# Batch 0's sketches with tokens stationary, a block-diagonal kv and a late division, in a sketched-attention and FFN kernel

## The chip, the cores and the metric

The kernel runs on one core of a Trainium2 chip. The metric is the time of one execution in microseconds (us) on the device; smaller is better. The core has five engines that run side by side, each through its own list of instructions in order, and meet through semaphores: TensorE (PE in the profile; its weight loads are the row PEld), VectorE (DVE), ScalarE (ACT), GpSimd (POOL) and SyncE (SP, which here only starts DMA transfers). SBUF is the working memory of 128 partitions; PSUM, in eight banks, receives TensorE's results.

## What is computed

Four batches of attention with polynomial sketches, then a feed-forward network over all 4352 tokens:

```
q, k, v: [4 batches, 4 heads, 1088 tokens, 32]    S1, S2: [8, 32]
phi(x) = (S1 x) outer (S2 x)                      -> 64 features per token
q_p, k_p = phi(q), phi(k)
kv  = sum over tokens of k_p (x) v                -> [batch, head, 64, 32]
z   = sum over tokens of k_p
num = q_p . kv        den = q_p . z + 1e-6
x   = (num / den), heads side by side             -> [4352, 128]
h   = x @ w_in        [128, 2048]
out = (h - tanh(h)) @ w_out     [2048, 128]
```

Inputs and output are float32. The denominator is not taken from the 64 features: with the Gram matrix of k's two sketches, den is a sum of eight products per token and head.

## The kernel before

**An order written out by hand.** Every operation is recorded with `P.add(engines, function, r=..., w=..., name=...)`. A long string, `TABLE` (line 26), then lists the operations in the order in which they are to stand: a number (the operation), a letter (v VectorE, a ScalarE, g GpSimd, t TensorE, s SyncE) and the buffer picked. `plan` (line 175) reads it, and `sync` (line 238) adds the semaphore waits that the data need. The tokens `f` and `F` are filler matmuls on zeros (lines 429 and 430), which write a bank that nobody reads. So the table decides which engine takes an operation and what stands in front of it; nothing is moved at run time.

**Names.** An operation's name says its step and batch. `kT0` are the transposes of k (line 536), `stt` that of S1 and S2 (542), `wab`, `wqd`, `wqc` the arranged S weights (545 to 555), `ksk0` the k sketch (581), `kab0` its move to SBUF (593), `gram0`, `gm0`, `scmm0`, `wqs0`, `sc0` the denominator's weights (608 to 638), `w0.0` to `w0.2` the products of the k sketches in three thirds (648), `kvmm0` the sum over tokens (663), `kvd`, `kvt`, `kvb` copies and a transpose of kv (672 on). For q: `qT` (573), `qsk` (706 and 759), `abc` its transpose to SBUF, `m`, `den`, `rd`, `aq` the denominator, its reciprocal and the division (712 to 718, 776 to 784), `qp` the products, `qpT` their transposes, `num` the numerator (737 and 818), `x` the copy into `xT`, the FFN's input. For the weights: `wi0` to `wi3` and `wo0` to `wo3` are casts to bf16, `wit` transposes of `wi` on TensorE (887), `wiT` their copies, `wc` a product of the two weights (901), used for the linear part of h - tanh(h). In the FFN, `h3.5` is group 3, block 5 of the first matmul (923), `th` the tanh on ScalarE (927), `dg` a part of h - tanh(h) on VectorE (932), `o` the second matmul (944, 948), `ot` and `st` the last transpose and store. Loads are `lk`, `lq`, `lv`, `lwi`, `lwo`, `sin` (line 465); `lv0.2` is the third load of v in batch 0.

**Stages.** The 4352 tokens go through the FFN in ten groups of columns (`GCOLS`: 384, 352, 352, six of 512, 192); each has 16 blocks `h`, 16 tanhs and 18 `o` matmuls. Group 0 needs only the first 384 columns of batch 0. Those are the first 12 of q's 34 token blocks, which `q_heads` (line 698) treats apart from the rest so that `h0.0` can start before the other tokens are through. The attention of batches 1 to 3, and the rest of batch 0 (`q_front(0, 3, 9)`), is interleaved with the FFN by the table.

**Batch 0's k side before** (line 575 on): the weights `wab` stay in the array and k streams through; the sketch comes out with features in partitions, and two VectorE transposes bring tokens back into partitions (`kab0.0`, `kab0.1`). Then the three products, three parts of `kvmm0`, and two ways out of the result: `kv_heads` (690) makes the block-diagonal form that the first numerator takes (`kvh`, a transpose, and `kve`, a product with a mask), `kv_tail` (672) the form that the rest takes (`kvd0`, `kvt0`, `kvb0`).

**Batch 0's first q before**: one matmul `qsk0.0`, a transpose `abc0.0`, then `m0.0`, `den0.0`, `rd0.0`, `aq0.0`: the quotient goes into one sketch factor ahead of the products `qph0`.

**The lock.** Operations with `lock=True` on VectorE and GpSimd are kept apart: each waits for the last locked one on the other engine (line 228). So two such products never run at the same time.

**Loads.** A load marked big waits until at most `CAP` (1.45 MB) is under way. Before, the first S load is issued by ScalarE, all others by SyncE.

Of the kernel before, what the change touches and what calls it, by code (L numbers as in the profile page):

```python
# [4 lines left out]
B, H, S, D = 4, 4, 1088, 32  # L5
# [5 lines left out]
NB = 9  # L11
# [15 lines left out]
0v 56g 16s 15a 10g 1g 18s 58g 2g 17s 4v 30s 19s 29s 21s 23s 50v:0 51v 20s 5v 52v 22s 54v 53v 55g f F F F F F F F F F F  # L27
66t:0 6v 64g 24s 67t 12g 65g 68t 60g 69v:0 3g 13g 25s 70v 57g f F F F 71t:0 84v 76g:0 26s 107v 72a:0 f F 73t 74a 27s
8g 77v:1 7g F F F 85t:0 35s 75v 78g:2 111t:0 86v:0 79t:1 112v:1 80t 87g:0 81t 9g 88v:0 113g:1 34s 229a 82v 89v:0 59g
90g:0 114v:1 108a:0 28s F F F F 109t 230a 91v:0 237t:0 95v:1 49s 231a 238t 115v:1 83v 240t:1 31s 232a 92v:0 116g:1  # L30
239a 96v:1 F 241t 117g:2 32s 110v:0 93t:2 242a 97t:1 33s 94a 124v:0 98a f F F 249t:0 125v 233g 251t:1 42s 253t:2
250a:0 38s 126t:0 118v:0 119g:0 252a:1 254a:2 255t:0 43s 281t:0 127v:1 257t:1 256a:3 282t 40s 283t 128v 259t:2 234g
258a:4 261t:0 120v 41s 129t:0 260a:5 263t:1 61g 235g 284t 39s 130a:1 265t:2 262a:6 285t 131t 14g 264a:7 286t 236v
267t:0 37s 266a:8 287t 269t:1 288t 132v:0 268a:9 134v:3 289t 243t:2 270a:10 271t:0 244t 36s 273t:1 135v:4 272a:11 290t
245t 274a:12 275t:0 121t:0 105s 136v:0 276a:13 103s 159v:0 277t:0 44s 279t:1 123a 246t 46s 133v 160v 278a:14 137t:2
247a 45s 138t 122v 139t 248v 161t:0 106s 143v 140a:1 280a:15 48s 304t:0 291t 141t 162v:0 305a:16 104s 292t 306t:1 163v
308t:0 142a:1 310t:2 144t:0 307a:17 169g:1 309a:18 100s 312t:0 311a:19 314t:1 293t 101s 145v:0 313a:20 316t:2 294t
295t 315a:21 296t 47s 318t:0 317a:22 320t:1 297t 319a:23 298t 146g:0 322t:2 164t:0 321a:24 299v:0 324t:0 323a:25
326t:1 147v:0 300s 165a:0 328t:2 325a:26 166t 336t:0 148v:0 327a:27 99s 337t 330t:0 167v:1 329a:0 149v:0 332t:1 102s
338t 331a:1 339t 168v 150g:1 178v 301s 334t:2 340t 333a:2 341t 359t:0 302s 335a:28 361t:1 342t 360a:29 363t:2 303s  # L40
179t:0 362a:3 152g:2 151v:1 364a:30 365t:0 343t 367t:1 344t 366a:31 180v:1 369t:2 345t 368a:4 371t:0 154g:0 346t
370a:5 373t:1 347t 372a:32 348t 375t:2 153v 349t 374a:33 377t:0 350t 376a:6 351t 181g:1 379t:1 352t 378a:7 155v 381t:2
380a:8 383t:0 353t 382a:9 385t:1 156t:0 354v:1 384a:10 386a:11 182v:1 355s 356s 391t:0 357s 392t 158v 157a 387t:0 393t
358s 389t:1 394t 388a:12 171v:2 414t:2 395t 390a:13 416t:0 415a:14 396t 418t:1 183v:1 397t 194v:0 417a:15 398t 184g:1
420t:2 399t 419a:16 422t:0 195v 185g:1 400t 401t 421a:17 424t:1 213v 402t 403t 423a:18 404t 426t:2 405t 425a:19 406t
170g:3 428t:0 427a:20 407t 408t 430t:1 429a:21 432t:2 409v:2 196t:0 431a:22 186v:0 410s 62g 187g:2 433a:23 434t:0 411s
436t:1 197v:1 438t:2 435a:24 412s 172t:2 198v 437a:25 173t 413s 204g:4 199t:0 439a:26 174t 200a:1 440t:0 201t 175v:0
442t:1 441a:27 446t:0 11g 202v:0 444t:2 63g 203v 176t 443a:0 189g:0 188v 447t 469t:0 445a:1 448t 471t:1 177v:2 470a:2
449t 473t:2 472a:28 205g:0 475t:0 190v 214t:0 474a:29 476a:3 477t:1 479t:2 215v:0 206g:1 450t 478a:30 451t 481t:0
480a:31 483t:1 452t 482a:4 453t 485t:2 454t 484a:5 216v:0 455t 487t:0 486a:32 217v:0 489t:1 191t:0 488a:33 218v:0  # L50
490a:6 219v:0 220g:1 491t:0 192v 493t:1 495t:2 492a:7 456t 457t 193v 222g:2 494a:8 497t:0 458t 496a:9 459t 221v:1
499t:1 460t 498a:10 524t:2 461t 224g:0 500a:11 223v 462t 463t 525a:12 527t:0 530t:1 464v:0 207t:0 528a:13 208t 526v
531a:14 465s 533t:2 529v 501t:0 466s 532v 502t 534a:15 225v 536t:0 467s 503t 539t:1 537a:16 504t 468s 535v 505t
540a:17 538v 542t:2 506t 545t:0 541v 543a:18 507t 548t:1 546a:19 508t 544v 509t 549a:20 551t:2 547v 510t 511t 552a:21
550v 554t:0 512t 557t:1 553v 555a:22 513t 560t:2 558a:23 514t 556v 515t 561a:24 563t:0 559v 516t 517t 564a:25 562v
566t:1 518t 569t:2 565v 567a:26 209t 519v:1 570a:27 599t:0 568v 520s 572t:0 571v 600a:0 602t:1 573t 521s 605t:2 603a:1
601v 574t 522s 575t 606a:2 608t:0 604v 576t 523s 577t 609a:28 607v 611t:1 578t 614t:2 610v 612a:29 579t 580t 210v:1
617t:0 615a:3 581t 613v 582t 618a:30 583t 616v 620t:1 584t 619v 623t:2 621a:31 585t 626t:0 624a:4 586t 622v 587t
627a:5 588t 625v 629t:1 211t 628v 632t:2 630a:32 589t 212v:3 635t:0 633a:33 226t:0 631v 636a:6 634v 590v:2 638t:1 637v
591s 647t:0 228a 227v 641t:0 592s 644t:2 639a:7 648t 593s 649t 642a:8 670t:0 640v 671t 594s 645a:9 674t:1 643v 650t  # L60
# [269 lines left out]
def bass_polysketch_attn__then__act_tanh_shrink_kernel(  # L330
# [311 lines left out]
    wvs = {}  # L642
# [399 lines left out]
```

## Time and profile before

| | us |
|---|---|
| median of 3 timed runs | 105.1 (104.66 to 106.0) |
| span of the profiled execution | 102.0 |
| start of the first FFN matmul in it | 17.28 |
| last FFN matmul issued | 98.33 |

The span runs from the first to the last instruction that the profile holds; the timed runs are longer by what lies around it. The profile lists, for each engine, groups of instructions with their busy time, their mean duration in ns, and how long the engine sat idle in front of them and for whom. A duration is that of one instruction from start to end. TensorE's matmuls are pipelined, so its rate is read from the distance of their starts: two 512-column bf16 matmuls start 216 ns apart, two 384-column ones 162 ns. A float32 matmul shows as two instructions, called passes here. On VectorE and ScalarE an instruction starts some 0.07 to 0.11 us before the one in front has ended; the distance of starts is called the pitch.

When the loads of batch 0 and of the weights landed, in us from the start of the span, from the trace's semaphores:

```
k, first half 3.34   second half 4.35     S1 3.69   S2 4.53
q, first part 6.27   second part 5.82 and 6.73
v, by heads   7.68, 8.02, 8.40, 10.96
w_in quarters 12.02, 12.69, 13.29, 13.95
w_out, first quarter 16.95
```

The S loads were issued at 0.74 (ScalarE) and 1.65 us (SyncE) and took 0.64 and 0.68 us to issue.

### The profile page before, as it was taken

Reading aid. Unit: us, or ns where it says so; the run is one execution under the profiler, and the core shown is the slowest. Engines: PE = TensorE matmul, PEld = TensorE weight load, DVE = VectorE, ACT = ScalarE, POOL = GpSimd, SP = SyncE. Lnnn points to the kernel's source line nnn. Section 1 sums busy time; section 2 is a strip of 40 time slices with the busy share of each in tenths; the row PEclk is TensorE's granted clock in tenths of the full one; section 3 lists DMA queues with packets and bytes.
Section 4 is the critical chain, followed back from the end, with each engine's and each line's share of the span. In section 5 each row is a group of like instructions: output and inputs, shape, how many; then the busy total and the mean of one; then the engine's idle time right before and its main releaser. Section 6 shows DMA issues by size and latency. Waiting matters only on the chain.

```text
span 102.0 us, 3040 instructions
## 1 busy us (share of the span) xinstructions
PE 96.4 (94%) x1260; PEld 48.4 (47%) x1260; DVE 79.7 (78%) x145; ACT 79.1 (78%) x157; POOL 35.8 (35%) x54
## 2 busy tenths in 40 slices
PE   5989889999999999999999999999999999999960
PEld 2343556476645454545634454444454444445650
DVE  1668899699948996977787789687899789999430
ACT  4001297996589996999899697999997999999940
POOL 3066939900053891299893880000000000000000
PEclk9999999999999999999999999999999999999999
DMA  2897999989995831303100004305100320601555
GB/s 90 230 291 171 318 310 262 297 263 325 313 278 174 237 58 21 48 8 53 24 0 6 0 0 63 46 0 79 24 0 10 55 45 0 98 5 17 82 75 81
DMA packets 25917, 11.37 MB, mean 111 GB/s; under 512 B 19120, under 2 KB 23600, under 8 KB 25904
## 3 DMA queue, kind: packets, MB, share of 16 engines
q1 hardware_dynamic: 24288, 10.98, 41.6%
q10 hardware_dynamic: 1616, 0.20, 1.3%
q8 instruction: 10, 0.16, 0.7%
q14 instruction: 3, 0.02, 0.1%
HBM read 8.95 MB, written 2.23 MB: 110 GB/s over the span
## 4 chain that ended last, share of the span: by engine, by line
PE 68%; POOL 12%; DVE 11%; DMA 3%; issue 2%; SPq 0%; DVEq 0%
PE psb L923 25%; PE psb L944 25%; POOL w L648 6%; POOL qp L802 4%; PE psb L818 4%; PE psb L581 3%; DMA kL<-in_k_dram 3%; PE psb L663 3%; PE psb L948 2%; PE psb L759 2%; PE psb L737 2%; DVE ot L953 2%; DVE qT L573 1%; DVE qp L724 1%; DVE rd L782 1%
## 5 line engine op out<-in xcount | busy, mean ns | idle before, releaser
L923 PE MATMUL psb<-xT,wi 128*128 128x512 bf16 (+3 forms) x160 | 48.8, 349 | 0.2 <-DVE th L932 0.2
L927 ACT ACTIVATE th<-psb 128x512 bf16<-128x512 f32 (+3 forms) x77 | 40.4, 598 | 2.7 <-PE psb L923 2.2
L944 PE MATMUL psb<-th,wo 128*128 128x512 bf16 (+3 forms) x90 | 26.4, 343 | 0.0
L923 PEld LDWEIGHTS psb<-xT,wi 128*128 128x128 bf16 x160 | 14.7, 97 | 23.1 <-ACT th L927 4.1
L927 ACT ACTIVATE wo_f<-psb 128x512 bf16<-128x512 f32 (+2 forms) x28 | 16.6, 629 | 1.5 <-PE psb L923 1.3
L802 POOL TENSOR_TENSOR qp<-ap,abc 128x768 f32<-128x768 f32 x11 | 16.5, 1514 | 3.7 <-DVE ap L784 3.5
L927 ACT ACTIVATE wi_f<-psb 128x512 bf16<-128x512 f32 (+3 forms) x31 | 16.6, 622 | 0.9 <-PE psb L923 0.7
L932 DVE TENSOR_TENSOR th<-psb,th 128x320 bf16<-128x320 f32 (+2 forms) x24 | 13.4, 565 | 1.9 <-ACT th L927 1.2
L648 POOL TENSOR_TENSOR w<-abk 128x768 f32<-128x768 f32 x7 | 10.6, 1516 | 9.2 <-DVE abk L593 8.2
L944 PEld LDWEIGHTS psb<-th,wo 128*128 128x128 bf16 x90 | 8.8, 100 | 5.2
L807 DVE STREAM_TRANSPOSE qpT<-qp 128x768 f32<-128x768 f32 x11 | 10.4, 956 | 0.8 <-POOL qp L802 0.8
L944 PE MATMUL psb<-wo_f,wo 128*128 128x512 bf16 (+1 forms) x32 | 10.9, 363 | 0.0
L944 PE MATMUL psb<-wi_f,wo 128*128 128x512 bf16 (+2 forms) x38 | 10.3, 344 | 0.0
L953 DVE STREAM_TRANSPOSE ot<-psb 128x512 f32<-128x512 f32 (+3 forms) x10 | 6.3, 628 | 3.4 <-PE psb L944 3.3
L430 PE MATMUL psb<-zz 128*128 128x512 bf16 x24 | 8.1, 465 | 0.0
L932 DVE TENSOR_TENSOR wi_f<-psb,wi_f 128x192 bf16<-128x192 f32 (+1 forms) x12 | 6.1, 510 | 1.6 <-ACT wi_f L927 0.9
L932 DVE TENSOR_TENSOR wo_f<-psb,wo_f 128x320 bf16<-128x320 f32 (+2 forms) x12 | 6.8, 572 | 0.7 <-ACT wo_f L927 0.3
L536 DVE STREAM_TRANSPOSE kT<-kL 128x576 f32<-128x576 f32 (+3 forms) x10 | 5.8, 605 | 1.5 <-DMA kL<-in_k_dram 1.4
L764 DVE STREAM_TRANSPOSE abc<-psb 128x1152 f32<-128x1152 f32 (+1 forms) x4 | 5.1, 1274 | 1.9 <-PE psb L759 1.8
L818 PE MATMUL psb<-qpT,kvb 32*32 32x288 f32 (+1 forms) x256 | 6.1, 392 | 0.0
L663 PE MATMUL psb<-w,vL 128*32 128x64 f32 x288 | 5.2, 221 | 0.3 <-DMA vL<-in_v_dram 0.3
L573 DVE STREAM_TRANSPOSE qT<-qL 128x1088 f32<-128x1088 f32 (+2 forms) x5 | 5.2, 1055 | 0.0
(89 smaller groups left out, 98.2 us busy)
## 6 DMA issues: line engine op xcount, KB each, us to landing
vL<-in_v_dram SPq DMA_DIRECT2D x16, 144.0 KB, 4.0
kL<-in_k_dram SPq DMA_DIRECT2D x8, 272.0 KB, 3.3
qL<-in_q_dram SPq DMA_DIRECT2D x6, 272.0 KB, 4.6
wi_f<-in_moe_w_in_dram SPq DMA_DIRECT2D x4, 256.0 KB, 5.6
wo_f<-in_moe_w_out_dram SPq DMA_DIRECT2D x4, 256.0 KB, 5.0
out_dram<-ot SPq DMA_DIRECT2D x14, 64.0 KB, 2.0
out_dram<-ot SPq DMA_DIRECT2D x8, 48.0 KB, 2.8
qL<-in_q_dram SPq DMA_DIRECT2D x2, 176.0 KB, 3.4
```

Of the source, the lines that this page charges most:

```text
L430: "F": lambda e, n: e.matmul(bank(3), zz.ap[:, 0:128], zz.ap[:, None, 128:384].to_broadcast([128, 2, 256]), start=True, stop=True)}, zop)
L573: P.add(_v((z - a) * 32), lambda e, n: e.transpose(tv.ap, vals[0].ap), r=vals, w=[tv] if b < 3 else [x[2] for x in qTv[0][1:]], name=f"qT{ ...
L648: P.add({**_v(768), **_gt(768)}, lambda e, n: e.tensor_tensor(out=wv.ap.rearrange("p (x i j) -> p x i j", i=8, j=8), in0=abh(0)[:, :, :, N ...
L663: i = e.matmul(pv[b].ap[h * 32:(h + 1) * 32, 0:64], vL[b][:, h, blk * 32:(blk + 1) * 32], wvs[b, p].ap[:, (bi * 4 + h) * 64:(bi * 4 + h + ...
L802: P.add({**_v(cn * 256), **_gt(cn * 256)}, lambda e, n, qp=qp, c0=c0, cn=cn: e.tensor_tensor(out=qp.ap[:, 0:cn * 256].rearrange("p (x i j) ...
L807: P.add(_v(cn * 256), lambda e, n, qp=qp, o0=o0, cn=cn: e.transpose(qt.ap[:, o0 * 256:(o0 + cn) * 256], qp.ap[:, 0:cn * 256]), r=[qp], w=[ ...
L818: i = e.matmul(psa4[h * 32:(h + 1) * 32, g, 0:nb * 32], kvb.ap[g * 32:(g + 1) * 32, x, h * 32:(h + 1) * 32], qq[g * 32:(g + 1) * 32, 0:nb, ...
L923: P.add(_mm(n_), lambda e, n, jb=jb, hv=hv: e.matmul(hv.ap[:, jb % m * 512:jb % m * 512 + n_], wi[jb // 4].ap[:, (jb % 4) * 128:(jb % 4 + ...
L927: act = P.add(_a(n_ * m), lambda e, n, hv=hv, th=th: e.activation(out=th.ap.rearrange("p (u x) -> p u x", u=m)[:, :, 0:n_], in_=hv.ap.rear ...
L932: P.add(_vp(gc * m), lambda e, n, hv=hv, th=th: e.tensor_tensor(out=th.ap.rearrange("p (u x) -> p u x", u=m)[:, :, 0:gc], in0=hv.ap.rearra ...
L944: fn = lambda e, n, x=x, st=st, sp_=sp_: e.matmul(ov.ap[:, 0:n_], wo[x // 4].ap[:, x % 4, :], ths[x][0].ap[:, ths[x][1] * 512:ths[x][1] * ...
L953: P.add(_vp(n_), lambda e, n: e.transpose(ot.ap[:, 0:n_], ov.ap[:, 0:n_]), r=[ov], w=[ot], name=f"ot{gi}")
```

## The change

1. **k sketch of batch 0** (`sketch0`): k's blocks of 32 tokens become the stationary operand and the S weights `wqdc`, block-diagonal over the heads, the moving one, 64 columns at a time. The result has tokens in partitions. 36 matmuls in three parts `kst0.*`, each followed by a copy from PSUM to SBUF (`kab0.*`; parts 0 on VectorE, 1 and 2 on ScalarE). The k transposes write k in another layout, for all batches; the sketches of batches 1 to 3 read it in one run.
2. **Products** (`outer0`, `qph0`): on VectorE the first factor is read from PSUM, and such a product no longer takes part in the lock. `lock` becomes a list of engines. `w0.0` is on VectorE, `w0.1` and `w0.2` on GpSimd; one of the two `qph0` is on each. `scx` and `dg` lose the lock too.
3. **kv** (`kv0`): v's blocks move and `w` is stationary, so that the sum is formed block-diagonal at once, after one matmul of zeros that clears the bank: 72 matmuls in three parts, a copy `kvd0` (ScalarE). `kvh` and `kve` are gone. The other form is made by one float32 matmul `kvr0` with a matrix of ones and zeros (`ehf`, built by `eh` on VectorE and `ehf` on ScalarE) and the copy `kvb0`.
4. **First q** (`q_heads`): 48 matmuls `qab0` and 48 `csk0` with tokens stationary replace `qsk0.0` and the transpose `abc0.0`. The products take the undivided sketch; the reciprocal is brought into the numerator's layout by a transpose (`rdt0`) and multiplied in when the numerator is copied out (`x0.0.*`, both on VectorE).
5. **Loads**: S2, one load of v (`lv0.2`) and two of w_in (`lwi0`, `lwi2`) are issued by ScalarE; the other three loads of v go ahead of q's second part on SyncE. `stt` no longer waits for a k transpose.
6. **The table** is new as a whole. There are 13 fillers and `kvz0` (the matmul of zeros) instead of 28 fillers. Of the four `wit`, only `wit1` stands ahead of `h0.0`. On VectorE `stt` is the first transpose, ahead of those of k; `abc0.3` stands ahead of the two `x0.0`. On ScalarE the order is `kab0.2`, `gm0`, `wqs0`, `lwi2` (behind q's second part), `wi0`, `kvd0`, `wi1`, `th0.0`, `th0.1`, `wi2`, `th0.7`, `th0.4`, `wi3`. `wiT0` and `wiT1` move from ScalarE to VectorE; of the products of batches 1 to 3, six go from GpSimd to VectorE and five the other way.

The diff, cut to its core:

```diff
-            if o.lock and e in lastl:
+            if e in o.lock:
                 d = lastl["gpsimd" if e == "vector" else "vector"]
...
-                    kTv[b][r0].ap.rearrange("p (j u t r) -> p r j u t", u=2, t=32, r=2)[:, r0:r1, e_:9, e_, :],
+                    kTv[b][r0].ap.rearrange("p (j t r u) -> p r j t u", u=2, t=32, r=2)[:, r0:r1, e_:9, :, e_],
...
+    def sketch0():
+        for p in range(3):
+            def sk(e, n, p=p):
+                for blk in range(3):
+                    for c in range(4):
+                        i = e.matmul(pk0[p].ap[c * 32:(c + 1) * 32, blk * 64:(blk + 1) * 64],
+                                     kTv[0][0].ap[:, ((p * 3 + blk) * 4 + c) * 32:((p * 3 + blk) * 4 + c + 1) * 32], wqdc.ap, start=True, stop=True, skip_group_check=True)
+                return i
...
+    def outer0():
...
+                a = sbuf if n == "gpsimd" else pk0[p].ap[:, 0:192].rearrange("p (k x i) -> p x k i", x=2, i=8)
...
+            P.add({**_vp(768), **_gt(768)}, mul, r=[pk0[p], ab0v[p]], w=[wv], name=f"w0.{p}", lock=("gpsimd",))
+
+    def kv0():
...
+                for x in range(2):
+                    for h in range(4):
+                        i = e.matmul(pvd.ap[h * 32:(h + 1) * 32, x * 128 + h * 32:x * 128 + (h + 1) * 32],
+                                     wvs[0, p].ap[:, (bi * 4 + h) * 64 + x * 32:(bi * 4 + h) * 64 + (x + 1) * 32],
+                                     vL[0][:, h, blk * 32:(blk + 1) * 32],
+                                     start=False, stop=(blk == 8), skip_group_check=True)
...
+        P.add(_pe(480, 185.0), lambda e, n: e.matmul(
+            pr.ap[:, 0:256], ehf.ap, kvd0.ap.rearrange("p x c -> p (x c)"), start=True, stop=True),
+            r=[kvd0, ehf], w=[pr], mode="128x128", name="kvr0")
...
+        def sk(e, n, dst, f0, f1):
+            for c in range(nx):
+                for h in range(H):
+                    i = e.matmul(dst.ap[h * 32:(h + 1) * 32, c * (f1 - f0):(c + 1) * (f1 - f0)], qt_.ap[:, c * 32:(c + 1) * 32],
+                                 wqd[:, h, f0:f1], start=True, stop=True, skip_group_check=True)
+            return i
...
+        P.add(_v(nx * 32), lambda e, n: e.transpose(
+            rdt.ap, rd.ap[:, 0:nx, None].to_broadcast([128, nx, 32])), r=[rd], w=[rdt], name="rdt0")
...
+            ot_p.seed(2, P.add(_vp((z - a) * 32), lambda e, n, a=a, z=z, xv=xv, pn=pn: e.tensor_tensor(
+                out=xv.ap, in0=pn.ap[:, 0:(z - a) * 32], in1=rdt.ap[:, a * 32:z * 32], op=ALU.mult),
+                r=[pn, rdt], w=[xv], name=f"x0.0.{j}"))
```

## The prediction

> **What bounds the kernel now.** I read the page's shares and slices, then the busy time in three stages, then the chain of waits up to the first FFN matmul (`h0.0`, 17.28 us), then single engines inside that stretch.
>
> The first two fences are from the page and from busy time by stage (columns: stretch and its length, then busy us and instructions of PE, PEld, DVE, ACT, POOL, then PEclk, DMA share, GB/s).
>
> ```profile
> PE 96.4 (94%) x1260; PEld 48.4 (47%) x1260; DVE 79.7 (78%) x145; ACT 79.1 (78%) x157; POOL 35.8 (35%) x54
> ...
> PEclk9999999999999999999999999999999999999999
> DMA  2897999989995831303100004305100320601555
> ```
> ```profile
> 0.00:17.28 17.28, 15.30 (x222) 7.68 (x223) 12.58 (x31) 6.57 (x12) 9.29 (x29) 1.00 0.79 237
> 17.28:25.00 7.72, 7.72 (x141) 4.53 (x141) 6.70 (x12) 6.33 (x16) 3.21 (x6) 1.00 0.94 295
> 25.00:98.40 73.40, 73.20 (x901) 36.17 (x899) 60.02 (x103) 66.23 (x130) 23.32 (x20) 1.00 0.29 63
> ```
>
> Behind `h0.0` TensorE is never idle for long: 80.9 of 81.1 us busy, while ACT has 8.5 us of slack. In front of it TensorE's 15.3 us are mostly fillers (28 on zeros) while it waits. So the time is when `h0.0` starts, plus TensorE's work behind it, plus a tail (last transpose and store) of 3.6 us, which the change leaves alone. The next fence is the chain of waits (start, us, what):
>
> ```profile
> 6.91 0.45 DVE abk L593
> ...
> 7.44 1.52 POOL w L648
> 8.98 0.97 DVE w L648
> 10.02 1.51 POOL w L648
> 11.54 0.34 POOL m L712
> ...
> 12.06 0.59 POOL m L776
> ...
> 13.13 1.03 DVE qp L724 x2
> ...
> 15.19 1.69 PE psb L737 x8
> ```
>
> Three batch-0 products run one behind the other over POOL, DVE, POOL, because locked products on the two engines wait for each other; the denominators queue behind them on POOL. Then come q's products, transposes and the numerator. Last, ACT and TensorE rows in order of time:
>
> ```profile
> 12.05 0.62 ACT L359 CAST wi<-wi_f 128x512 bf16<-128x512 f32 x1 [3.38 <-DMA wi_f<-in_moe_w_in_dram]
> 12.57 0.37 ACT L359 COPY kvd<-psb 128x256 f32<-128x256 f32 x1
> ```
> ```profile
> 7.41 0.34 PE L608 MATMUL psb<-abk 128*32 128x32 f32 x17
> ...
> 11.01 1.21 PE L663 MATMUL psb<-w,vL 128*32 128x64 f32 x72 [0.27 <-DMA vL<-in_v_dram]
> ```
>
> The first pair shows that wi arrived only at 12 us. From the second come prices: 72 passes of 64 columns start within 1.21-0.22 = 0.99 us (14 ns each), 17 of 32 columns within 0.34-0.20 = 0.14 us (9 ns each).
>
> **The front, step by step** (new starts in span time).
>
> *S and k.* Both S loads are now issued by ACT, 0.64 us each, the second at 1.4. S landed 2.9 us after its issue before (3.7 and 4.5), so now at 4.3; k's halves landed at 3.35 and 4.35. The S transpose now stands first on DVE, ahead of all k transposes, two of which ran at 3.4 before. So everything behind it begins at 4.3: S (pitch 0.17), `wqd`, newly on DVE (0.17), and four k transposes (pitch 0.40, 0.33, 0.40, 0.33) end at 6.15, against 5.46. I charge this in full: the sketch starts at 6.2, not 5.51. If S lands at 3.7, it starts at 5.4.
>
> *k sketch.* 36 matmuls, two passes each like L663, 64 columns: 72 x 14 ns = 1.0 us, ready in thirds at 6.8, 7.1, 7.45. Plain copies (0.33 us, row 128x192 from PSUM) replace two transposes: `kab0.1` on ACT to 7.2, `kab0.0` on DVE to 7.5, `kab0.2` on ACT, behind a DMA issue and `ehf`, to 8.0.
>
> *q's first sketch.* `qab0` is 48 matmuls of 16 columns, `csk0` 48 of 8. No row has these; nearest are 9 ns a pass at 32 columns, 14 at 64. I take 9: 96 x 9 = 0.85 us each. Bounds 0.6 and 1.35; the upper would delay `h0.0` by about 0.5 each. [...]
>
> *Products.* `w0.0` on DVE reads one factor from PSUM. Price: 768 elements took 0.96 us from SBUF, L932's 640 with a PSUM factor 0.82, the same rate. It runs 7.55 to 8.5 without the lock. POOL makes `w0.1` 7.3 to 8.8 and `w0.2` to 10.3 (1.51 each): last product 10.3, not 11.54. No row shows such products side by side; the bounds are 0 and one whole DVE product (+1.0). I take 0: beside DVE's transposes L573, L709 and L764 POOL's w stayed at 1.51, those being single-stream too.
>
> *kv.* 72 matmuls of 32 columns: 144 x 9 = 1.3 us in thirds; the last, behind `csk0` and `w0.2`, gives its result at 11.4. This replaces 0.99 us, the transpose `kvh` (0.25) and the mask `kve` (0.36). v was whole at 10.96 before; its loads now go ahead of q's second part, and three fourths had landed by 8.4 even before: I take 8.4, not binding. `kvd0` copies on ACT (0.37) to 11.9.
>
> *Numerator.* Unchanged at 1.69 us: 12.0 to 13.7. m, den, rd and the new `rdt0` (0.55, like L730) cost 1.3 us of DVE, beside kv and numerator. But DVE is FIFO: `abc0.3` (0.99), then two dividing copies (0.33 each) end at 14.25. Loads moved from SP to ACT free SP by 0.5 to 0.6 us each and add a wait: `lwi2` stands on ACT until q's second part lands, with `wi0` and `kvd0` behind it; `kvd0` also stands behind the cast of wi's first quarter. If that lands by 11, nothing is lost; it is issued at about 7 on a queue of its own, not 6.5 behind v, and I take 11. `h0.0` at 14.4: **2.9 us earlier**.
>
> **What is paid behind it.** Three of four wi transposes (before, all lay in the waits of the front) come behind `h0.0`: 3 x 4 x 56 ns plus weights = 0.72 us. `kvr0`, a 256-column f32 matmul, replaces `kvt0` and is also behind: two passes at 163 ns x 256/192, plus 0.1 of a first load and 0.09 of a mode switch = 0.53. **+1.25 us.** ACT now casts wi2 and wi3 (0.52 pitch) among the first tanhs (0.385 pitch against 0.32 of TensorE for an h and an o), and POOL reaches wo0 only after qp. By order, TensorE waits for batch 1's k transpose (0.6), tanhs (0.7) and x0.3 (0.3) soon after: 1.2 to 1.6 us. Before, all its waits behind `h0.0` came to about 1.3 us (kvmm 0.6, qsk1 0.4), nearly all after 25 us, and that part is reordered. I take +0.4 net, between 0 and +1.5. Fewer POOL products and the new kT layout: 0, since `ksk` keeps its 8 matmuls of 288 columns (0.76 us now; bound -0.1 for all three).
>
> **Sum:** -2.9 + 1.25 + 0.4 = -1.25 us; span 102.0 to 100.8. The profiled span stands 3.1 below the median of 105.1; with the same 3.1 around it, 103.85, rounded to **103.8 us**.
>
> **Rivals.**
> 1. *Charges not met* (0.34). S lands at 3.7: -0.8. Or tanh pacing leaves TensorE gaps that the wi transposes fill: -0.7 to -0.95. For: a small load's 2.9 us may be mostly waiting beside k's stream; ACT's pitch exceeds TensorE's. Against: both earlier S loads took the same 2.9; the new order has its own waits. One of them gives 103.0, both 102.2.
> 2. *Weights bind* (0.10): wi's first quarter lands at 12.0 as before, `kvd0` ends at 12.95, numerator 13.05 to 14.75, `h0.0` at 15.2. For: v's last fourth and wi straggled then, at 130 GB/s from 8.5 to 10 us. -2.1 + 1.25 + 0.4: 104.7.
> 3. *Slower: the clock falls* (0.16). The first fillers start 427 ns apart and, from 4.75 us, 216: TensorE ran at half speed for its first 3.6 busy us. After 5.3 us the change drops all but two of 17 fillers, and the front's matmuls, in 128*32 tiles, load the array less than fillers do. If the clock falls at about 8 us, the 2.3 us of `qsk0.3` and numerator double, the small matmuls perhaps too (+1.9), and the FFN's first 3.6 us do half their work (+1.8): +4.1 to +6.0, net +2.9 to +4.8, about 109. It decides if the clock is still down at `h0.0`. Against: no gap of the new order exceeds about 1 us, and the row never leaves full speed. [...]
> 4. *The products don't overlap* (0.04), so the freed lock does nothing: `h0.0` at 15.4, 104.8. For: two streams each; against: the transposes above.
>
> **Numbers.** Forecast 0.36, its own range 102.8 to 104.9. From 2% (103.0 and 107.2; about what runs of 104.66 to 106.0 can tell): faster is a quarter of the forecast, 0.10, and most of rival 1, 0.29: 0.39. Slower is most of rival 3, 0.15, and 0.01 of rival 2's tail: 0.16. Within: 0.45. The range 101.8 to 106.8 leaves out rival 3 and the edge of rival 1.
>
> **What would show it.** `stt` at 4.3 and the first sketch at 6.2; passes of 9 ns; POOL's two w back to back at 1.51 beside DVE's; `h0.0` at 14.4 (15.2 with `kvd` standing behind `wi`: rival 2); 216 ns between 512-column matmuls throughout; TensorE waits of 1.2 to 1.6 us soon after `h0.0`. Wrong if `h0.0` comes after 15.5, or waits behind it grow by over 1.5 us.

## The result: 116.4 us, slower, and the profile after

| | before | after |
|---|---|---|
| median of the timed runs, us | 105.55 (104.66 to 106.16) | 116.38 (116.15 to 116.75) |
| span of the profiled execution | 102.0 | 114.3 |
| first FFN matmul `h0.0` starts | 17.28 | 26.19 |
| from there to the start of the last `h` matmul | 79.97 | 82.84 |
| the rest of the span | 4.75 | 5.27 |

The ratio is 1.105 (95% interval 1.097 to 1.113). Of the 12.3 us between the spans, 8.9 came in front of `h0.0`, where 2.9 were to be saved, and 2.9 behind it, where 1.65 were forecast. The last 0.5 lies in the tail, which the prediction took as unchanged.

The first fence is from the page of after, in the order of the one before: busy time of the engines, the granted clock and the DMA share by slices, and the queue that carries instructions. The second is busy time by stage, with the columns of the prediction's second fence.

```profile
PE 99.2 (87%) x1548; PEld 52.4 (46%) x1548; DVE 83.3 (73%) x149; ACT 79.5 (70%) x157; POOL 34.2 (30%) x50
...
PEclk9999755558999999999999999999999999999999
DMA  3988499899850000004026300400700410014455
...
q8 instruction: 12, 0.20, 0.8%
```
```profile
0.00:26.19 26.19, 16.43 (x496) 11.03 (x497) 11.01 (x29) 4.07 (x9) 7.02 (x26) 0.75 0.82 253
26.19:45.00 18.81, 17.80 (x327) 10.21 (x327) 16.03 (x27) 15.98 (x41) 11.86 (x13) 0.99 0.34 106
45.00:110.00 65.00, 64.59 (x726) 31.05 (x725) 55.92 (x94) 59.45 (x108) 15.34 (x12) 1.00 0.22 36
```

Three things stand here. TensorE ran 496 matmul records and 497 weight loads in front of `h0.0`, where before had 222 and 223. The clock, at full speed in the row of before throughout, is at half from 13.1 to 26.75 us. And no other engine was busy for even half of the front. The chain of waits of after shows what the time goes to (start, us, what):

```profile
1.43 3.73 DMA sin<-in_S_dram
...
6.04 1.48 DVE kT L544 x3
...
7.57 1.21 PE psb L697 x72
...
10.42 0.27 PE psb L727 x7
10.69 2.63 issue
...
15.22 2.65 issue
...
20.34 1.69 issue
22.02 0.86 PE psb L815 x6
22.88 2.87 PE psb L792 x8
```

Three times TensorE waits in the middle of an operation for nothing that the profile shows: 2.63 + 2.65 + 1.69 = 6.97 us. Its data were there. The timeline around the first gap (start, us, engine, operation, idle before) shows POOL finishing its products meanwhile and `kvmm0` (L727) picking up where it had stopped, after 10 records of a run that all had their inputs:

```profile
10.05 1.51 POOL L712 TENSOR_TENSOR w<-abk 128x768 f32<-128x768 f32 x1
...
10.41 0.28 PE L727 MATMUL psb<-vL,w 128*32 128x32 f32 x10
...
13.32 0.39 PE L727 MATMUL psb<-vL,w 128*32 128x32 f32 x13 [2.63 <-issue]
```

Counting the trace's TensorE records in order of start (matmuls, weight loads, and the few records of TensorE's own semaphore waits, 7 of the 1000 in front of `h0.0`) gives the places. The gaps lie right behind the 449th, the 705th and the 961st record: 256 apart. The instruction queue q8 moves packets of 16,384 bytes, and one lands shortly ahead of the end of each gap. There are 12 of them in this execution and 10 in that of before, as many as there are marks (records 194, 450, 706 and so on, 256 apart) in their 3115 and 2539 records:

```
                            after                     before
record 194 starts           8.66                      10.17
record 450 starts          13.32  (gap 2.63)          17.03  (no gap)
record 706 starts          17.87  (gap 2.65)          24.14  (no gap)
record 962 starts          22.02  (gap 1.69)          28.86  (no gap)
q8 packets                 10.95-11.84, 15.45-16.50,  11.96-12.93, 17.88-18.86,
                           19.52-20.62, 23.77-25.40   26.51-27.39, 30.39-32.07
h0.0 is record             1001                       452
```

TensorE resumes 1.48, 1.37 and 1.40 us after a packet's end; in every run below that has a gap at such a mark, it resumes 1.3 to 1.5 us after one. In after the first four packets start 2.29, 2.13, 1.65 and 1.75 us behind the records 194, 450, 706 and 962, in before 1.79, 0.84, 2.37 and 1.53. So the author's reading, from these counts and times alone: a packet is a block of 256 of TensorE's instructions; a packet goes with each mark that TensorE passes; and where TensorE reaches the next mark before the block has landed, it stands. What lies between the queue and TensorE the trace does not show. Before ran 256 records in 4.7 to 7.1 us, and every block was in time, the closest by 1.47 us (27.39 against 28.86). The sketches of after run 256 records in about 2 us (8.66 to 10.69), and every block up to `h0.0` is late.

Theory A was that reading: records per microsecond against blocks, with the lower clock as its consequence. The rivals: the clock falls for want of work and is itself the main loss; the late start of the sketch (7.57 against 5.51 us) is; or the rest of the chain (loads, products, a new order) is.

### The profile page after: what moved, and what is told of

Read it like the earlier page. It is cut to its first block, busy times and chain, and to the rows that moved or that the text cites. A ratio compares the mean times of both kernels' runs of the same rounds, so it can differ in the third digit from the quotient of the medians.

```text
span 114.3 us, 3613 instructions
## 1 busy us (share of the span) xinstructions
PE 99.2 (87%) x1548; PEld 52.4 (46%) x1548; DVE 83.3 (73%) x149; ACT 79.5 (70%) x157; POOL 34.2 (30%) x50
## 4 chain that ended last, share of the span: by engine, by line
PE 73%; DVE 9%; issue 7%; POOL 4%; DMA 3%; ACTq 1%; ACT 0%
PE psb L977 25%; PE psb L998 24%; DVE kT L544 6%; PE psb L874 4%; PE psb L815 3%; DMA sin<-in_S_dram 3%; PE psb L665 3%; POOL qp L858 3%; PE psb L792 3%; PE psb L1002 2%; PE psb L756 2%; PE psb L727 2%; PE psb L589 1%; PE psb L697 1%; DVE xT L360 1%
## 5 line engine op out<-in xcount | busy, mean ns | idle before, releaser
L981 ACT ACTIVATE th<-psb 128x512 bf16<-128x512 f32 (+3 forms) x78 | 43.2, 596 | 9.4 <-PE psb L977 8.8
L981 ACT ACTIVATE wo_f<-psb 128x512 bf16<-128x512 f32 (+3 forms) x29 | 17.2, 610 | 1.3 <-PE psb L977 1.0
L986 DVE TENSOR_TENSOR th<-psb,th 128x320 bf16<-128x320 f32 (+2 forms) x26 | 14.6, 566 | 3.2 <-ACT th L981 2.5
L858 POOL TENSOR_TENSOR qp<-ap,abc 128x768 f32<-128x768 f32 x8 | 12.0, 1512 | 1.3 <-DVE qp L858 1.1
L998 PE MATMUL psb<-wi_f,wo 128*128 128x512 bf16 (+2 forms) x33 | 11.5, 355 | 0.0
L998 PE MATMUL psb<-wo_f,wo 128*128 128x512 bf16 (+2 forms) x36 | 10.9, 342 | 0.0
L544 DVE STREAM_TRANSPOSE kT<-kL 128x576 f32<-128x576 f32 (+3 forms) x10 | 8.7, 936 | 0.0
L986 DVE TENSOR_TENSOR wo_f<-psb,wo_f 128x192 bf16<-128x192 f32 (+2 forms) x10 | 5.7, 568 | 1.1 <-ACT wo_f L981 0.6
L986 DVE TENSOR_TENSOR wi_f<-psb,wi_f 128x192 bf16<-128x192 f32 (+2 forms) x12 | 6.0, 507 | 0.4
L815 PE MATMUL psb<-qT,wq 32*32 32x288 f32 (+1 forms) x128 | 4.1, 441 | 1.7 <-issue 1.7
```

The lines of the kernel that those rows point to most:

```text
L544: P.add(_v(nb * 32 * (r1 - r0)), lambda e, n, e_=e_, nb=nb, r0=r0, r1=r1: e.transpose(kTv[b][r0].ap.rearrange("p (j t r u) -> p r j t u", ...
L815: i = e.matmul(psa4[g * 32:(g + 1) * 32, h, 0:sn], wq[h * 32:(h + 1) * 32, :], qv4(b)[h * 32:(h + 1) * 32, s0:s1, g, :], start=True, stop= ...
L858: P.add({**_v(cn * 256), **_gt(cn * 256)}, lambda e, n, qp=qp, c0=c0, cn=cn: e.tensor_tensor(out=qp.ap[:, 0:cn * 256].rearrange("p (x i j) ...
L981: act = P.add(_a(n_ * m), lambda e, n, hv=hv, th=th: e.activation(out=th.ap.rearrange("p (u x) -> p u x", u=m)[:, :, 0:n_], in_=hv.ap.rear ...
L986: P.add(_vp(gc * m), lambda e, n, hv=hv, th=th: e.tensor_tensor(out=th.ap.rearrange("p (u x) -> p u x", u=m)[:, :, 0:gc], in0=hv.ap.rearra ...
L998: fn = lambda e, n, x=x, st=st, sp_=sp_: e.matmul(ov.ap[:, 0:n_], wo[x // 4].ap[:, x % 4, :], ths[x][0].ap[:, ths[x][1] * 512:ths[x][1] * ...
```

## Experiments

Each median is compared with runs of before on the same chip, whose medians were 105.0, 104.7, 104.5 and 104.8 in the four batches.

**1. After, with q's two sketches in wide matmuls** (`e1_wide_q`), 360 records fewer:

```diff
-            for c in range(nx):
-                for h in range(H):
-                    i = e.matmul(dst.ap[h * 32:(h + 1) * 32, c * (f1 - f0):(c + 1) * (f1 - f0)], qt_.ap[:, c * 32:(c + 1) * 32],
-                                 wqd[:, h, f0:f1], start=True, stop=True, skip_group_check=True)
+            w_ = H * (f1 - f0)
+            for c in range(nx // 4):
+                i = e.matmul(dst.ap[:, c * w_:(c + 1) * w_], qt_.ap[:, c * 128:(c + 1) * 128],
+                             wqd[:, :, f0:f1], start=True, stop=True, skip_group_check=True)
```

> The changed kernel with q's two sketches in 3 + 3 wide matmuls (128 tokens stationary, all four heads at once) in place of 48 + 48 small ones: the same products, 360 fewer TensorE records ahead of h0.0, which comes as about the 640th instead of the 1000th. The values of batch 0's first 384 tokens land in another layout, so those output rows are not the reference's.
> Theory A (TensorE runs out of fetched instructions; each of the three gaps of 2.6, 2.7 and 1.7 us stands where another 256 instructions are needed): one gap is left, at the 449th record; the other two go. h0.0 between 18.5 and 21.5 us instead of 26.2, time 108 to 111.5 us against 116.4.
> Theory B (the small tiles or the clock hold TensorE, the gaps are its restart): the clock falls as before, gaps stay in number though not in place; 114.5 to 117 us.
> Theory C (the chain of S, w0 and kvd0 is late, TensorE merely waits for it): h0.0 stays at 25.5 to 26.5, 115.5 to 117 us.

Measured: three runs of 108.97 to 109.39 us and one of 106.8. In the profiled one (108.97) `h0.0` starts at 19.16 instead of 26.19, as record 641, and no gap is left at a mark of 256: record 450 comes only 3.9 us after record 194. That is A, and `h0.0` comes seven microseconds earlier. What stays is the clock, in the page's slices and in TensorE's timeline:

```profile
PEclk9995555999999999999999999999999999999999
```
```profile
5.15 0.27 PE L433 MATMUL psb<-zz 128*128 128x256 bf16 x1
7.41 1.10 PE L697 MATMUL psb<-wqd,kT 128*32 128x64 f32 x54 [1.98 <-DVE kT L544]
```

The 1.98 us in which TensorE waits for k's transposes lie in the stretch from 4.71 to 8.12, behind which the clock is at half until 18.36. The run of 106.8 kept the full clock; the other three had a mean of 0.952. So, by that one run, the clock costs this kernel 2.4 us, and without either fault it stands 1.8 us above before.

**2. Before, with many small matmuls added** (`e2_more_small`): each filler from the 12th on becomes a short filler and 16 matmuls of 32 columns on zeros, 544 records more.

```diff
+        i = plain["f"](e, n)
+        for j in range(16):
+            g = j % 4
+            i = e.matmul(bank(3)[g * 32:(g + 1) * 32, 256:288], zz.ap[:, 0:32], zz.ap[:, 0:32], start=True, stop=True, skip_group_check=True)
```

> The kernel before, with each of the 17 fillers behind the first 11 cut to half its columns and followed by 16 matmuls of 32 columns in 32-column tiles: 544 more records in the first 17 us, nothing else changed, no result changed. Each filler lasts about as long as before (0.1 us of columns and 16 passes of about 9 ns).
> Theory A: idle stretches of TensorE that wait for nothing, right behind the 449th, the 705th and perhaps the 961st record, 1 to 2.7 us each; h0.0 at 20 to 25 us instead of 17.3; 108.5 to 114 us against 105.5.
> Theory B: small tiles cost their own passes only; h0.0 17.3 to 17.8, 105.3 to 106.2 us.
> Theory C: the kernel before has the early S and the old chain, so nothing moves: 105.3 to 106 us.

Measured: 110.61 us, ratio 1.044 (1.035 to 1.052). The chain of waits:

```profile
10.38 0.21 PE psb L429
10.60 0.20 PE psb L441 x13
10.79 2.45 issue
13.24 0.20 PE psb L441 x3
```

The 449th record, done at 10.79, brings a gap of 2.45 us in a kernel in which nothing else of the change is present, and the 705th one of 0.59. `h0.0` moves from 17.28 to 23.81, but the gaps are only 3.0 of these 6.5 us. The added work has a price of its own: a short filler and its sixteen matmuls start 0.42 us from the next such pair, where one filler took 0.22. And the clock, at half from 14.30 to 17.71 us, has `kvmm0` take 2.15 us instead of 1.21. So the place and the length of the gaps speak for A, not the whole of the delay. A holds from both sides: take records away and the gaps go, add records and they come.

**3. After, with records spent early** (`e3_burn_early`): 8 small matmuls behind each of the first 11 fillers, 176 records in a stretch that was meant to be one where TensorE only waits.

> The changed kernel with 8 small matmuls added behind each of the first 11 fillers: 176 more records before 5.5 us, when TensorE has nothing else to do; no result changed.
> Theory A, with the next block asked for when the 193rd record is passed: that is passed at about 5.5 us instead of 8.7, so the third block is there at about 10 instead of 13.3, and the gaps come earlier in the program: h0.0 2 to 3 us earlier (23 to 24.5 us) with more instructions, time 113 to 114.5 us against 116.4. (A with blocks that are never asked for early, only missed: a fourth gap, 117.5 to 119 us.)
> Theories B and C: 0 to +0.3 us.

Measured: 115.4 us, ratio 1.097 (1.090 to 1.103). The gap at 449 is gone (its block came at 7.91 to 8.79), but those at 705 and 961 are 2.01 and 3.81, and `h0.0` is at 25.70: a gain of 0.5 us, where 2 to 3 had been expected. The records were not spent early: a filler with its eight took 0.71 us where a filler alone had taken 0.43, so the 194th record started at 9.02 instead of the 5.5 that was expected, and the k sketch at 9.08 instead of 7.57. The clock also rose later, with its first entry at full at 11.31 (after: 6.27), and the sketch took 2.1 us instead of 1.2. From record 706 to record 962 it then took 5.1 us. That `h0.0` came no later although the sketch began 1.5 us later agrees with A; as a test of what early records are worth, the run says little.

**4. After, with k's sketch in wide matmuls** (`e4_wide_k`), 9 of 128 tokens instead of 36 of 32, 108 records fewer.

> The changed kernel with k's sketch in 9 matmuls of 128 tokens in place of 36 of 32: the same values in the same places, 108 fewer records, so that h0.0 comes as about the 892nd, ahead of the 961st, where the third gap was.
> Theory A: gaps at the 449th and the 705th record alone, both 108 records later in the program; h0.0 at 22.5 to 24.5 us, time 112.5 to 114.8 us against 116.4.
> Theory B: the small tiles of the k sketch took 1.0 us, the wide ones take about as long: 115.8 to 116.6 us.
> Theory C: 116 to 116.6 us.

Measured: 116.07 us (114.04 to 116.59), a miss. Gaps of 0.60 at 449 and 4.26 at 705, none at 961; `h0.0` at 26.45. Record 450 started at 15.49, and the next block began to arrive only at 19.36. The clock was at half from 8.50 to 25.57. One run had a mean clock of 1.0 and still took 116.59 us, which speaks against the clock as the main loss. Why that block took so long stays open.

**5. After with wide q sketches and the clock held up** (`e5_hold`): experiment 1 with 8 more fillers in front of the sketch.

> The kernel of e1_wide_q (batch 0's first 384 tokens again in another layout, so those rows are not the reference's) with 8 more full fillers behind the first 10, so that TensorE is busy where it idled from 5.4 to 7.4 us while it waited for k's transposes. In e1 three runs of four had a mean clock of 0.952 and took 109.0 to 109.4 us, one had 1.0 and took 106.8; in the profiled one the clock was half from 8.1 to 18.4 us.
> If the clock falls for the idle stretch ahead of the sketch and costs 2.4 us: full clock in every run, 106.3 to 107 us. If the clock's fall has no price of its own (the work waits for the other engines anyway): 108.5 to 109.4 us whatever the clock. If the eight fillers delay the sketch: up to +0.2 us on either.

Measured: 107.83 us, ratio 1.028 (1.022 to 1.035). The clock stays full; one gap of 0.86 us is left at 449. `h0.0` starts at **16.40, 0.9 us earlier than before**: with few records and a full clock the front does save time. What ends last is no longer TensorE (chain of waits):

```profile
7.91 5.50 DMA wi_f<-in_moe_w_in_dram
...
13.44 0.62 ACT wi L360
14.06 0.28 ACT kvd L360
...
14.39 1.58 PE psb L792 x8
```

wi's first quarter lands at 13.42, and `kvd0` stands behind its cast: the prediction's rival 2, in the place that it named. From `h0.0` to the last `h` matmul it took 83.4 us, against 79.97 before, and behind that 6.1, against 4.75; this eats the gain.

**6 and 7. k's transposes ahead of `stt`** (`e7_wide_q_kt_first` on experiment 1, `e8_kt_first` on after), in the table: `55v 51v:0 ... 53v` becomes `51v:0 52v ... 53v 55v`, with the S weights behind it.

> The kernel of e1_wide_q (same rows in another layout) with the transpose of S and what hangs on it put behind three of k's four transposes on VectorE, as the kernel before has it; in the changed kernel they wait for S, which lands at 5.15 us, and the sketch starts at 7.6 us instead of 5.5.
> Theory A with the clock's fall as a part of its own: sketch at 6.1 to 6.4 us, TensorE idle under 1 us before it, clock full in most runs; 105.3 to 106.8 us; a gap of up to 1.5 us at the 449th record may come back, since the 193rd is passed earlier and the third block is not there sooner than about 4.3 us after it.
> Theory C (the late start is the main loss): 1.5 us less than e1 at the same clock, 105.3 us, and no gap.

> The changed kernel, whole and with the reference's values, with the transpose of S behind three of k's four transposes on VectorE: the sketch starts about 1.4 us earlier.
> Theory A: the three gaps stay, at the 449th, 705th and 961st record, each about 1.2 us earlier in time and as long as before; 114.8 to 115.6 us against 116.4.
> Theory C: the late chain is what costs; h0.0 comes 1.5 to 3 us earlier and the gaps shrink: 113 to 114.5 us.
> If blocks come at times that do not depend on when they are asked for: 116 to 116.8 us.

Measured: 108.52 us (ratio 1.034, 1.027 to 1.041) and 116.14 us (1.112, 1.105 to 1.118). Both sketches started about 1 us earlier (6.33 and 6.46). The second kernel gained nothing from it; the first is 0.6 us below experiment 1, within the spread of its runs (107.75 to 110.56). In the second, TensorE resumes at 13.39, 17.95 and 22.09; in after at 13.32, 17.87 and 22.02. The gaps had grown by what the start had won. Of that run's expectations this is the third, and not A's, which had the gaps move forward with the start: its 194th record started 1.0 us earlier than in after (7.65), but the first packet came no earlier (11.06 against 10.95). In the first kernel's profiled execution, the longest of its four, there is now a gap of 4.14 us at 449, where experiment 1 had none. So a late sketch is not what the change lost its time by: blocks set the times.

**8. Before with only part of the change, few records** (`c2_few_records`): k's sketch wide with tokens stationary, a product with a PSUM factor beside POOL's, the late division; kv, q's sketch and the loads as before. Batch 0's k tokens stand in another order than v's here.

```diff
+                    i = e.matmul(pk0[p].ap[:, blk * 64:(blk + 1) * 64],
+                                 kTv[0][0].ap[:, (p * 3 + blk) * 128:(p * 3 + blk + 1) * 128], wqdc.ap, start=True, stop=True, skip_group_check=True)
...
+            P.add(_vp(768) if p == 0 else _gt(768), mul, r=([pk0[p]] if p == 0 else []) + [ab0v[p]], w=[wv], name=f"w0.{p}", lock=("gpsimd",))
...
+                in0=pt(0, a, z)[:, :, :, None].to_broadcast([128, z - a, 8, 8]),
```

> The ideas of the change with few TensorE instructions, in the kernel before: k's sketch with tokens stationary in 9 wide matmuls (36 records where the kernel before has 64), the first product on VectorE from PSUM beside two on GpSimd, q's sketch and kv as in the kernel before, the division behind the first numerator, S loaded and transposed as in the kernel before. The reference's values.
> Theory A: no gap at the 449th record (it lies behind h0.0), clock full from 5 us on, h0.0 at 15 to 16 us instead of 17.3, then a wait of o0.0 for wo0, which lands at 17.0 and is cast by 17.6 us: 103.5 to 104.8 us against 105.0.
> If tokens stationary, the products with a PSUM factor or the late division are themselves what cost the changed kernel its time: 106 us or more.

Measured: 106.95 us, ratio 1.023 (1.018 to 1.028). No gap, full clock, `h0.0` at 18.51. The group of the wide sketch (busy us, mean ns, idle):

```profile
L601 PE MATMUL psb<-wqd,kT 128*128 128x64 f32 x18 | 2.6, 309 | 0.0
```

18 wide passes take 2.6 us, where after's 72 narrow ones take 1.0. Up to 6.55, where the clock's first entry at full lies, they start 0.22 us apart, behind it 0.11; at full clock throughout they would need some 2.0 us, an estimate from that distance. So for TensorE the narrow form took less time here, where no gap stood in it. The wide form frees the front of gaps and gives up part of the gain; TensorE also waits 1.38 us for `kvd0` here, so the 1.2 us by which `h0.0` is later aren't the sketch's alone.

**9. After with one large load at a time** (`e9_one_load`), to measure a block with quieter queues. The total is that of weights that come late.

```diff
-                    left = CAP - o.dma[0]
+                    left = (CAP if len(loads) < 10 else 3e5) - o.dma[0]
```

> The changed kernel, with the reference's values, in which from the eleventh load on (the weights wi and wo, and the later batches) a load is issued only when the one before it has landed, where up to 1.45 MB are under way otherwise. The front then has the DMA queues nearly to itself from about 10 us on.
> Theory A, and that a block of instructions waits in the DMA engines behind the data: the instruction packets start about 1 us after they are asked for (0.7 us in the quiet stretch at 34 us) instead of 1.7 to 2.3 us, and the three gaps shrink from 2.6, 2.7 and 1.7 us to about 1.5 us and less each; h0.0 at 22.5 to 24.5 us instead of 26.2. What the whole then takes is open, since the weights come later (110 to 120 us).
> Theory A with a fetch that takes its time whatever the load: the gaps stay at 2.4 us and more.
> Theories B and C: the gaps stay as they are.

Measured: 146.62 us, ratio 1.402 (1.395 to 1.408); the front is what counts. TensorE's timeline at its gaps:

```profile
13.32 0.51 PE L727 MATMUL psb<-vL,w 128*32 128x32 f32 x36 [1.14 <-issue]
...
16.77 0.23 PE L756 MATMUL psb<-wqd,qT 128*32 128x8 f32 x3 [1.99 <-issue]
...
20.10 0.85 PE L815 MATMUL psb<-qT,wq 32*32 32x192 f32 x6 [0.87 <-issue]
```

From mark to mark (9.87, 13.32, 16.77, 20.10) 256 records took 3.45, 3.45 and 3.33 us; in after 4.66, 4.55 and 4.15. The DMA share in these stretches is 0.32 to 0.44, in after 0.72 to 0.90. The packets started 1.05 to 1.10 us behind the mark, in after 1.65 to 2.29. So a block costs about 3.4 us with quieter queues, and about 1 us more beside the data loads. The gaps shrink from 6.97 to 4.0 us; they do not go. `h0.0` came at 25.12, later than the 22.5 to 24.5 that were expected; the clock was at half from 14.12 to 27.78 us.

**10. Before without its 28 fillers** (`e10_no_fill`), which has of the change's two faults only the lower clock.

> The kernel before without its 28 fillers, matmuls whose results nobody reads: the same work in the same order, with the reference's values, but TensorE idle where they stood. It prices the clock by itself, with no gap for instructions (56 records fewer).
> If half clock in the front costs as much as e1's runs showed (2.4 us for 10.2 us of it): clock half until 15 to 21 us, h0.0 at 18.5 to 20 us instead of 17.3, 106.5 to 108.5 us against 104.8.
> If the front's matmuls are too few for the clock to matter there: up to +0.6 us, 104.8 to 105.5 us.

Measured: 106.06 us, ratio 1.012 (1.006 to 1.019). The clock by slices:

```profile
PEclk9999997599999999999999999999999999999999
```

The row shows the drop from 17.21 to 20.62 us. The trace's first clock entry, at full, is at 13.79 (before: 4.75); up to there `kvmm0` took 2.0 us of busy time instead of 1.2, and the numerator in the drop 2.8 instead of 1.7. The median rises by 1.6 us; in the profiled execution, the longest of the four, `h0.0` comes at 20.18, 2.9 us late. That is what a low clock in the front is worth here without the gaps: far from 11.

**11. Experiment 8 with the narrow k sketch** (`c3_few_records`), and after's layout of kT; `h0.0` is record 461.

> The ideas of the change in the kernel before once more, with k's sketch in small tiles (1.0 us for its 144 records in the changed kernel, where the 36 wide ones took 2.7 us in c2) and k's tokens in the changed kernel's order, which c2 lacked; the second half of batch 0's sketch is put behind the first numerator, and the division behind it. kv and q's sketch as in the kernel before. The reference's values.
> Theory A: some 530 records ahead of h0.0, so the 449th comes at 13 us or later, when the third block, asked for at about 8.5 us, is there: no gap over 0.5 us, clock full from 5 to 7 us on, h0.0 at 15.3 to 16.5 us: 103.5 to 105 us against 104.8.
> If tokens stationary, the products with a PSUM factor or the late division cost the time by themselves: 106 us or more.

Measured: 111.81 us, ratio 1.064 (1.058 to 1.070). `h0.0` starts at 16.71, 0.6 us earlier than before and without a gap at 449; but this order puts batch 1's k transposes behind a late `abc0.3`, and TensorE pays for it behind `h0.0` (timeline):

```profile
21.61 0.74 PE L577 MATMUL psb<-kT,wab 64*32 64x288 f32 x8 [2.44 <-DVE kT L532]
```

TensorE idles for 4.9 us between `h0.0` and the last `h` matmul, where before it did for 0.2. The longest of it, 2.45 us, is the wait shown, and no gap stands at the mark of 449, so what missed the expectation was the table's order and not a late block; the run says nothing else of the total.

**12. After with the old kT layout for batches 1 to 3** (`f1_k_layout`).

> The changed kernel with k transposed as before in batches 1 to 3 (two runs of 64 tokens instead of neighbours taken by turns; 64 columns are zeroed again ahead of each, 0.1 us); batch 0, whose tokens must stand together to be stationary, keeps the new layout. The reference's values. In the changed kernel a k transpose of 576 columns took 1.10 to 1.22 us, before 0.72 to 0.77, and TensorE waited 0.65 us for the first of them ahead of ksk1.
> If that layout is part of what the change costs behind h0.0: these transposes 0.7 to 0.8 us, the wait ahead of ksk1 gone or under 0.1 us, 0.4 to 1.0 us less, 115.4 to 116.0 us against 116.4.
> If TensorE only waits elsewhere then (for the weights, which come late anyway): 116.1 to 116.6 us.
> The front with its three gaps stays as it is in both.

Measured: 116.92 us, ratio 1.119 (1.104 to 1.134). A transpose of 576 columns took 0.72 us again, and from `h0.0` to the last `h` matmul the profiled execution took 82.0 us, against 82.84 in after. The profiled executions of experiments 1, 3, 4, 6 and 7, which keep the new layout, took 82.80 to 82.84 there, so the 0.8 us are more than the spread. But the front came out 0.5 us longer (gaps of 7.52 us), and the total shows no gain; it is inconclusive.

## Why the prediction was wrong, point by point

**The step that failed** is the price of the small matmuls: "I take 9: 96 x 9 = 0.85 us each" for q's first sketch, and "144 x 9 = 1.3 us" for kv. The passes were priced right by the row that was chosen; their number was not priced at all. L608's 17 passes at 9 ns say how fast TensorE runs narrow passes that it has. They do not say how fast instructions arrive, and 17 records can't. Four lots of narrow matmuls raise the records in front of `h0.0` from 452 to 1001, about two blocks more, all within the stretch that was to be shortened. At 4.2 to 4.7 us a block, as measured, the marks at 194, 450, 706 and 962 put record 962 at 8.66 + 4.66 + 4.55 + 4.15 = 22.02; experiment 7 reached the first of them 1.0 us earlier and still had record 962 at 22.09. Experiments 1, 2 and 9 show it. 3, 6 and 7 agree, in that a sketch that began later or earlier did not move the records behind the marks with it. Experiment 4 does not fit as well: with 108 records fewer it won nothing, because one block took longer than any in after.

**Rival 3, the clock**, came true in that the clock fell and was still down at `h0.0`. It had been held unlikely by "no gap of the new order exceeds about 1 us"; how long a gap lowers the clock no run had shown. The clock fell at 13.10, within the gap of 2.63 us (10.69 to 13.32), and stayed at half for 13.65 us, through the gaps of 2.65 and 1.69 us. Numerator 2.87 us instead of 1.69, `csk0` 1.49 instead of 0.85, `qsk0.3` 1.71 instead of 0.6: these are its marks. But while blocks set the pace, slower matmuls partly fill gaps that would be there anyway. An estimate from the trace: record 962 would stand near 22.02 in any case, so at full clock only what follows it (0.86 + 2.87 us) could shrink, by some 1.6 us; experiments 10 and 1 give 1.6 and 2.4. The clock alone was not taken out of after, so this split stays an estimate. The prediction priced it at 4.1 to 6.0 us, too much, and missed its cause. The longest single gap in front of a fall was 1.98 us in experiment 1, 2.45 in experiment 2 and 2.63 in after.

**The start of the sketch**: 6.2 forecast, 7.57 measured. S landed at 5.15, not 4.3 (3.73 us in flight, not 2.9), and k's transposes took 0.65 and 0.59 us each, not 0.48 and 0.40, because of the new layout. The prediction's "the new kT layout: 0" looked at its reader `ksk` and not at its writer. The groups of VectorE by shape (busy us, mean ns, idle), after and before:

```profile
L544 DVE STREAM_TRANSPOSE kT<-kL 128x576 f32<-128x576 f32 x3 | 3.6, 1206 | 0.0
...
L544 DVE STREAM_TRANSPOSE kT<-kL 128x288 f32<-128x288 f32 x2 | 1.3, 652 | 0.0
```
```profile
L536 DVE STREAM_TRANSPOSE kT<-kL 128x576 f32<-128x576 f32 x3 | 2.3, 751 | 0.0
...
L536 DVE STREAM_TRANSPOSE kT<-kL 128x288 f32<-128x288 f32 x2 | 1.0, 480 | 1.5 <-DMA kL<-in_k_dram 1.4
```

Since experiments 6 and 7 won nothing by an earlier sketch, this step cost after little; it would count once the records were few.

**Steps that held.** k's sketch took 1.0 us as forecast. `w0.0` with a PSUM factor ran on VectorE at 8.91 for 0.96 us while POOL's two ran back to back at 1.51 each, so the lock's end was worth what was said, and rival 4 fell. `qab0` took 1.0 us for 0.85.

**Weights.** "I take 11" for wi's first quarter was wrong too (12.6 in after, 13.42 in experiment 5), hidden in after by the gaps. Rival 2 had its place right.

**Behind `h0.0`**: 2.87 measured, 1.65 forecast. `wit` 1.2 us of busy time, sized at 0.72 (12 transposes near 0.1 each, not 0.06); `kvr0` 0.6 for 0.53 (the three terms given for it add up to 0.63; the 0.09 of a mode switch is an estimate: in before the last 128*32 pass and the 128*128 load behind it start 0.11 us apart, at 7.62 and 7.73); waits 1.2 more than before (1.41 against 0.20) where 0.4 were taken. The waits of after lie within the 1.2 to 1.6 that were forecast; what was wrong is the "about 1.3 us" taken off for before, where TensorE idled for 0.20 us behind `h0.0`. Of the 1.41, 1.14 stand in front of the k sketches of batches 1 to 3, whose transposes the layout slows. Experiment 12 has these waits down to 0.05, and 0.84 us less between `h0.0` and the last `h` matmul; but TensorE's idle time there was 1.53 us in all, so where the 0.84 was won isn't shown. Here only sizes were off. TensorE's timeline shows the largest:

```profile
28.65 0.72 PE L589 MATMUL psb<-kT,wab 64*32 64x288 f32 x16 [0.65 <-DVE kT L544]
```

**Is the idea sound without the records?** Experiment 5 says in part: `h0.0` 0.9 us earlier, not 2.9, and more than that given back behind it. No kernel of this study beat before.

## What to carry to other kernels

Count instructions as well as time: where a short critical stretch is cut into small matmuls, find out from the trace how many records lie between two arrivals of the instruction queue (256 here), and whether TensorE will reach the next mark before the block is there. A row with 17 fast passes prices a pass, not several hundred of them. And when a layout is changed for its reader, price its writer too.

## What the runs showed of the hardware

- In after and before, each 16,384-byte packet of the queue q8 goes with one of TensorE's records 194, 450, 706 and so on, 256 apart: 12 packets for 3115 records and 10 for 2539. A packet started between 0.75 us ahead of its record and 2.37 us behind it; at the first four marks of after it was 1.65 to 2.29 behind, in experiment 9 1.05 to 1.10, in experiment 4 once 3.87, and in experiment 3 once 1.1 us ahead; why isn't settled. Where TensorE stood at the next mark, it resumed 1.3 to 1.5 us after the packet's end. From mark to mark 256 records then took 3.3 to 3.5 us with one large load at a time (experiment 9) and 4.2 to 4.7 in after, which is 13 to 18 ns for each record (5.1 us once in experiment 3, 6.2 once in experiment 4), while the sketches of after ran 256 records in 2.03 us, 8 ns each. No run has such a gap up to its 449th record.
- Two changes of the granted clock lay 3.41 us apart in experiments 2 and 10, 6.83 and then 13.65 in after, 10.24 in experiment 1, 13.66 in experiment 9 and 17.07 in experiment 4; the shortest, 3.41, goes into the others a whole number of times. In the 3.41 us in front of a fall TensorE was idle for 1.98 us (experiment 1), 2.36 (experiment 2) and 2.51 (after). Idle time alone doesn't decide: the 3.41 us in front of those, from 6.27 to 9.69 in after, had 1.29 us of it and kept the clock, and those from 13.79 to 17.21 in experiment 10, with 1.24, lost it. In experiment 3 TensorE was busy almost without a break from 1.1 to 11.3 us, up to 9.1 with a filler and eight matmuls of 32 columns by turns, and the clock's first entry at full came only at 11.31.
- A VectorE transpose of f32 that writes its elements four apart in memory took longer than one that writes them two apart: 1.6 times for 576 columns (1206 ns in after against 751 in before) and 1.4 times for 288 (652 against 480). With the old layout back, in experiment 12, the 576 columns took 0.72 us.
- A VectorE product with one factor in PSUM ran beside GpSimd's without slowing it: in after `w0.0` took 0.96 us from 8.91 on, beside GpSimd's two from 8.57 on at 1.51 us each; in before, where the lock kept such products apart, GpSimd's took 1.51 and 1.52.
